# Attention into mixture of experts: router's 32-bit matmuls regrouped, scale sums in bfloat16, low halves of x queued after the maxima

## The chip, the cores and the metric

The kernel runs on one core of one Trainium2 chip. The metric is device time in microseconds (us), the median of several executions; a profile of one execution goes with it. Engines are called PE (TensorE), DVE (VectorE), ACT (ScalarE), POOL (GpSimd) and SP (SyncE, which here only issues DMAs).

## The reference

An attention over 8 batches and 8 heads (1152 keys, head size 64, queries averaged in pairs to 576 rows) feeds a router and eight experts. Every token goes to the expert with the largest logit.

```python
q_pool = q.reshape(B, H, S // factor, factor, D).mean(axis=3)
scores = scale * np.matmul(q_pool, k.transpose(0, 1, 3, 2))
scores = scores - np.max(scores, axis=-1, keepdims=True)
attn = np.exp(scores)
attn = attn / (np.sum(attn, axis=-1, keepdims=True) + 1e-09)
attn_out = np.matmul(attn, v)
...
logits = x @ w_gate
e_idx = np.argmax(logits, axis=1)
...
eom = 1.0 / (1.0 + np.exp(-(x @ w_output_gate)))
for e in range(E):
    mask = e_idx == e
    h = np.maximum(x[mask] @ w1[e], 0.0)
    out[mask] = gate_w[mask, None] * eom[mask, e, None] * (h @ w2[e])
```

Since the choice of the expert is discrete, the attention is computed to nearly 32-bit accuracy: operands are split into a high and a low 16-bit half, and the halves' products are added.

## The kernel before

The attention works on 32 pairs of heads, four pairs to a batch. A loop of steps (18 steps to a pair) writes, in each step, a piece of several generators, and the order in which it writes them is the order on PE, DVE, ACT and POOL (a hand-made order; only SP's DMAs are placed by the scheduler). A step holds:

- the scores of one block of 128 keys (lines 440 and 442) into one of two PSUM buffers `sps`, and their exponentials on ACT (444). In some steps ACT computes a second exponential (446) and DVE subtracts (449) to get the low half `pl`; in the others POOL does it (452);
- one or two row maxima of the next pair (generator `mgen`): two or three matmuls into a PSUM bank `mp` (377) and a DVE reduction (378). Even steps hold one maximum, odd steps two;
- in even steps a burst of up to three blocks of `av`, the product with the values (467 to 469), and at a head's end its division on DVE (476 to 478);
- preparation of the pair after next, by tables of (place, operation), three places to a step: `PREPK` for keys and queries, `PREPV` for values. In it `gk` (213) and `gmax` (319) add a column over the partitions by a 32-bit matmul with a block of ones, and DVE makes a power of two of the sum (218 to 223, 324 to 329). `FWD` moves tables against each other, `SLEAD` is how many steps early the preparation runs.

After a pair's second head the router's generator `logits` takes over, one piece in each even step. For the pair's 128 columns of x it transposes two, then three blocks into PSUM (523, called T2 and T3 here), copies the high half out on ACT (`xh`, 527), subtracts it on DVE for the low half (`xl`, 530), and multiplies both halves by the router's weights in 32-bit matmuls (540), for the columns 0 to 256 (540a) and 256 to 576 (540b) apart, which DVE adds up in `lT` (542, 544). After a batch's fourth pair `router` does the rest. `rows` transposes the maxima in 32 bits (412) once for each group of tiles.

All of 377, 213, 319, 412, 523, 540 and the router's later matmuls share three PSUM banks. `psum()` gives the bank that was given longest ago and isn't held; the writing matmul then waits until DVE or ACT has read what was in it. `psum(True)` holds a bank until `free` is called. Small DVE operations wait in a list `fill`, from which `pop` takes them at fixed points.

After the attention, 21 tiles of tokens go through the experts, in an order that waits for nothing of the above but the last batch's router.

Of the kernel before, what the change touches and what calls it, by code (L numbers as in the profile page):

```python
# [8 lines left out]
F32 = mybir.dt.float32  # L9
F32R = mybir.dt.float32r  # L10
F16 = mybir.dt.float16
BF16 = mybir.dt.bfloat16
# [15 lines left out]
         (78, 'amax', 0), (82, 'amax', 1), (99, 'gmax'), (100, 'scale', 0), (100, 'scale', 1), (100, 'scale', 2), (103, 'vh', 0), (103, 'vs', 0), (106, 'vh', 1), (107, 'vl', 0), (109, 'vs', 1), (113, 'vl', 1))  # L28
PREPK = ((0, 'lk'), (12, 'qsum'), (14, 'kabs'), (20, 'gk'), (21, 'ksc', 0), (22, 'ksc', 1), (23, 'ksc', 2), (25, 'ks', 0), (26, 'ks', 1), (27, 'kh', 0), (29, 'kh', 1), (29, 'kl'), (29, 'qs'), (30, 'dk', 0), (31, 'dk', 1), (31, 'qh'), (33, 'dq', 0), (34, 'dq', 1), (34, 'ql'), (37, 'qd'), (38, 'dl', 0), (40, 'dl', 1))
PREPV = ((63, 'lv'), (82, 'amax', 0), (88, 'amax', 1), (93, 'gmax'), (94, 'scale', 0), (95, 'scale', 1), (99, 'scale', 2), (100, 'vh', 0), (101, 'vs', 0), (103, 'vl', 0), (107, 'vh', 1), (107, 'vs', 1), (110, 'vl', 1))  # L30
FWD = 9
PREP = PREPK + tuple((r + FWD, *x) for r, *x in PREPV)
# [17 lines left out]
P32 = 10  # L50
SLEAD = 35
S = 1152
# [20 lines left out]
def attention(tc, qT, kT, vL, wg, keep, xrows, idscr, cum, pairs, setup, scat, init, exps):  # L73
    nc = tc.nc
    nb = len(pairs) // 4
    with ExitStack() as ctx:
# [16 lines left out]
        def psum(hold=False, name="tp"):  # L93

            while len(held) == 3:
                pop() if fill else pendv.pop(0)()
            k = next(i for i in banks if i not in held)
            free(k)
            if hold:
                held.add(k)  # L100
            x = ps_m.tile([128, 512], F32, name=name, tag=f"mp{k}")
            return (x, k) if hold else x
# [14 lines left out]
        blk = keep['blk']  # L117
# [25 lines left out]
        def prep(n, table):  # L143
# [67 lines left out]
            def gk():  # L211
                g, k_ = psum(True)
                nc.tensor.matmul(g[:, 0:1], lhsT=blk, rhs=ak[:, 0:1], start=True, stop=True)
                gk_.extend((g[:, 0:1], k_))
# [101 lines left out]
            def gmax():  # L316
                g, gk = psum(True)
                g = g[:, 0:2]
                nc.tensor.matmul(g, lhsT=onesf, rhs=am, start=True, stop=True)
                gm.extend((g, gk))  # L320
# [72 lines left out]
        def pop(k=1):  # L393
            while k and fill:
                fill.pop(0)()
                k -= 1
# [87 lines left out]

        routers = []

# [25 lines left out]
        def logits(b, c, xb):  # L512
# [4 lines left out]
            if b == nb - 1 and c == 3:  # L517
                idle(ps_s.tile([128, 512], F32, name="idle4", tag="sps0"), WARM[4])
            for c0, c1, grp in ((0, 256, (0, 1)), (256, NQ, (2, 3, 4))):
                tx, tk = psum(True)  # L520
                for i, t in enumerate(grp):
# [3 lines left out]
                for o, w in ((0, c1 - c0),) if c0 == 0 else ((0, 256), (320, 64)):  # L525
# [3 lines left out]
                    def sub(o=o, w=w, z=z, tx=tx, tk=tk if not d else None):  # L529
                        nc.vector.tensor_tensor(out=xl[:, z], in0=tx[:, o:o + w], in1=xh.bitcast(F32)[:, z], op=ALU.subtract)  # L530
                        if tk is not None:
                            free(tk)
                    fill.insert(0, sub)
                    d += w
                yield 1
            for c0, c1 in ((0, 256), (256, NQ)):
                pop(99)
                tl = psum()
# [147 lines left out]
        with tc.manual_schedule(engines={E.PE, E.DVE, E.Activation, E.Pool}):  # L686
# [19 lines left out]
            for s in range(18 * NP + 14):  # L706
# [8 lines left out]
                for r in routers:  # L715
                    if not s % 2 or not live or not r[1]:
                        r[1] = next(r[0], 0)
                pop()
                if live:
# [6 lines left out]
                adv('m', mg, mw)  # L726
                if s < 54 or s % 2 == 0:
                    rows()
# [6 lines left out]
                if not live:  # L735
                    pop(3)
            pop(99)
            for r in routers:
                for _ in r[0]: pass


def keep_tiles(tc, kp, NT, NP_):
# [8 lines left out]
    nc.vector.memset(t('onesf', [128, 128], F32), 1.0)  # L751
    blk = t('blk', [128, 128], F32)
    nc.gpsimd.memset(blk, 0.0)
# [502 lines left out]
```

## Time and profile before

| | us |
|---|---|
| median of 3 runs | 1487.44 |
| lowest and highest run | 1484.61, 1488.31 |
| profiled execution, whole time | 1491.79 |
| its span, first to last instruction | 1489.9 |
| PE busy in the span | 1431.0 |
| DVE, ACT, POOL busy | 1117.9, 1012.9, 939.1 |

A matmul's end in the profile is modelled: a row maximum's matmul of 384 columns is shown 0.33 us long, but in a dense stretch the next one starts 0.165 us after it. So PE's own time is read from start to start, and an idle time that the profile shows is some 0.16 us shorter than what was lost. PEld rows are weight loads, which overlap with matmuls. The attention takes up to about 983 us of the span, the experts the rest.

### The profile page before, as it was taken

Reading aid. Unit: us, or ns where it says so; the run is one execution under the profiler, and the core shown is the slowest. Engines: PE = TensorE matmul, PEld = TensorE weight load, DVE = VectorE, ACT = ScalarE, POOL = GpSimd, SP = SyncE. Lnnn points to the kernel's source line nnn. Section 1 sums busy time; section 2 is a strip of 40 time slices with the busy share of each in tenths; the row PEclk is TensorE's granted clock in tenths of the full one; section 3 lists DMA queues with packets and bytes.
Section 4 is the critical chain, followed back from the end, with each engine's and each line's share of the span. In section 5 each row is a group of like instructions: output and inputs, shape, how many; then the busy total and the mean of one; then the engine's idle time right before and its main releaser. Section 6 shows DMA issues by size and latency. Waiting matters only on the chain. (4 is left out here: it accounts for less than half of the span.)

```text
span 1489.9 us, 40217 instructions
## 1 busy us (share of the span) xinstructions
PE 1431.0 (96%) x16044; PEld 1144.2 (77%) x16044; DVE 1117.9 (75%) x2438; ACT 1012.9 (68%) x1723; POOL 939.1 (63%) x892
## 2 busy tenths in 40 slices
PE   7899999999999999999999999889999999999996
PEld 4677777777777777777777777777888888888874
DVE  8678787887887787788787787576778778777752
ACT  5777778777877877777877776644655556556542
POOL 3877888788889779878879888663333233333200
PEclk9999999999999999999999999999999999999998
DMA  5445344444443453444244433148636665453550
GB/s 190 123 122 145 102 134 123 115 118 118 117 137 102 115 143 98 117 134 121 86 137 125 126 92 96 58 148 330 231 105 232 228 233 213 171 186 122 218 186 8
DMA packets 92047, 212.57 MB, mean 143 GB/s; under 512 B 13356, under 2 KB 28924, under 8 KB 91854
## 3 DMA queue, kind: packets, MB, share of 16 engines
q1 hardware_dynamic: 81262, 188.35, 40.8%
q0 software_dynamic: 9152, 20.85, 4.1%
q8 instruction: 128, 2.10, 0.6%
q10 hardware_dynamic: 1440, 0.74, 0.2%
q14 instruction: 65, 0.53, 0.1%
HBM read 164.23 MB, written 23.02 MB: 126 GB/s over the span
## 5 line engine op out<-in xcount | busy, mean ns | idle before, releaser
L378 DVE TENSOR_REDUCE pm<-mp 128x1 f32<-128x384 f32 x864 | 449.5, 549 | 114.2 <-PE mp L377 109.6
L444 ACT ACTIVATE p<-sps 128x576 f32<-128x576 f32 x576 | 375.8, 653 | 199.6 <-PE sps L442 180.7
L452 POOL TENSOR_TENSOR pl<-p 128x576 f16<-128x576 f32 x383 | 437.8, 1146 | 112.5 <-ACT p L444 94.0
L377 PE MATMUL mp<-ka,qa 128*128 128x384 f16 x960 | 297.3, 326 | 12.0 <-DVE pm L378 6.5
L467 PE MATMUL av<-vt,p 128*128 128x65 f16 x2880 | 291.8, 193 | 0.2 <-DVE xb L478 0.2
L468 PE MATMUL av<-vt,p 128*128 128x64 f16 x2880 | 291.5, 194 | 0.0
L469 PE MATMUL av<-vt,pl 128*128 128x65 f16 x2880 | 291.1, 192 | 0.0
L467 PEld LDWEIGHTS <-p 128*128 128x128 bf16 x2880 | 265.8, 97 | 20.8 <-DVE xb L478 4.4
L468 PEld LDWEIGHTS <-p 128*128 128x128 bf16 x2880 | 264.4, 97 | 14.0
L469 PEld LDWEIGHTS <-pl 128*128 128x128 f16 x2880 | 264.3, 98 | 0.0
L377 PE MATMUL mp<-kb,qb 66*128 66x384 f16 x768 | 250.7, 326 | 0.8 <-DVE kb L251 0.5
L440 PE MATMUL sps<-qa,ka 128*128 128x288 f16 x1152 | 235.9, 286 | 11.2 <-DVE pl L449 9.8
L958 PE MATMUL hps<-x,w1h 128*128 128x512 f32 (+1 forms) x704 | 230.7, 389 | 7.6 <-DVE x L942 3.4
L442 PE MATMUL sps<-qb,kb 69*128 69x288 f16 x1152 | 235.7, 285 | 0.0
L449 DVE TENSOR_TENSOR pl<-sps,p 128x576 f16<-128x576 f32 x193 | 146.2, 757 | 38.1 <-ACT sps L446 29.8
L958 PE MATMUL hps<-x,w1l 128*128 128x256 f32 (+1 forms) x704 | 165.4, 276 | 0.0
L960 ACT COPY hs<-hps 128x512 f32<-128x512 f32 (+1 forms) x88 | 49.0, 557 | 171.0 <-PE hps L958 171.0
L958 PEld LDWEIGHTS hps<-x,w1l 128*128 128x128 f32 x704 | 132.3, 190 | 13.0
L958 PEld LDWEIGHTS hps<-x,w1h 128*128 128x128 f32 x704 | 122.8, 190 | 23.9 <-DVE x L942 4.0
L442 PEld LDWEIGHTS <-kb 69*128 69x128 f16 x1152 | 112.7, 98 | 29.2
L377 PEld LDWEIGHTS <-qa 128*128 128x128 f16 x960 | 95.2, 99 | 46.8 <-issue 9.5
L790 POOL DMA_INDIRECT ids<-idscr,riD x36 | 44.8, 1244 | 134.4 <-DMA out_dram<-y,ids 123.1
(243 smaller groups left out, 2810.5 us busy)
## 6 DMA issues: line engine op xcount, KB each, us to landing
raw2b<-in_w_dram SPq DMA_DIRECT2D x24, 1024.0 KB
raw1b<-in_w_dram SPq DMA_DIRECT2D x24, 1024.0 KB
raw1a<-in_w_dram SPq DMA_DIRECT2D x22, 1024.0 KB
raw2a<-in_w_dram SPq DMA_DIRECT2D x22, 1024.0 KB
vp<-in_vL_dram SPq DMA_DIRECT2D x32, 576.0 KB
qp<-in_qT_dram SPq DMA_DIRECT2D x31, 576.0 KB
kpf<-in_kT_dram SPq DMA_DIRECT2D x31, 576.0 KB
ka<-xk SPq DMA_DIRECT2D x120, 144.0 KB
```

The source lines that it names most:

```text
L377: nc.tensor.matmul(mp, lhsT=l, rhs=r, start=j == 0, stop=j == len(ops) - 1)
L378: nc.vector.tensor_reduce(out=pm[:, i:i + 1], in_=mp, axis=AX.X, op=ALU.max)
L440: nc.tensor.matmul(sps[:, j, 0:288], lhsT=ka[:, h, ks], rhs=qa[:, o + 288 * j:o + 288 * j + 288], start=True, stop=False)
L442: nc.tensor.matmul(sps[:, j, 0:288], lhsT=kb[:, h, ks], rhs=qb[:, h, 288 * j:288 * j + 288], start=False, stop=True)
L444: e_ = nc.scalar.activation(out=p32.rearrange("p (j n) -> p j n", j=2), in_=x, func=AF.Exp, scale=1.0 / 16)
L449: nc.vector.tensor_tensor(out=pl.rearrange("p (j n) -> p j n", j=2), in0=x, in1=ph.rearrange("p (j n) -> p j n", j=2), op=ALU.subtract)
L452: nc.gpsimd.tensor_tensor(out=pl, in0=p32, in1=ph, op=ALU.subtract)
L467: nc.tensor.matmul(av_[:, qb, 0:65], lhsT=hi, rhs=vt[:, h, c, 0:65], start=c == 0 and qb == 0, stop=False)
L468: nc.tensor.matmul(av_[:, qb, 0:64], lhsT=hi, rhs=vt[:, h, c, 66:130], start=False, stop=False)
L469: nc.tensor.matmul(av_[:, qb, 0:65], lhsT=lo, rhs=vt[:, h, c, 0:65], start=False, stop=c == NC - 1 and qb == 4)
L958: nc.tensor.matmul(hp[:, f, 0:n], lhsT=W1[l][g][:, c, fs], rhs=d['x'][:, c, 0:n], start=c == 0 and l == 0, stop=c == 3 and l == 0)
L960: nc.scalar.copy(out=hs, in_=hp[:, :, w:2 * w])
```

## The change

`gk` and `gmax` take the upper 16 bits of their 32-bit operand as bfloat16, and their ones are bfloat16. In `logits` T3 and 540a are issued in one piece; the subtractions go to a list `subs` that is emptied at the end of a step, after its maxima. `rows` is called, from step 54 on, right behind the router's piece. The K side of the preparation runs a step earlier (`SLEAD` 36, with `FWD` 12 holding the V side where it was), but its low half `kl` on POOL is put one place later than before, behind one more of the step's own subtractions.

```diff
-... (29, 'kh', 1), (29, 'kl'), (29, 'qs'), (30, 'dk', 0), ... (34, 'dq', 1), (34, 'ql'), (37, 'qd'), (38, 'dl', 0), (40, 'dl', 1))
+... (29, 'kh', 1), (29, 'qs'), (30, 'dk', 0), ... (34, 'dq', 1), (33, 'kl'), (35, 'ql'), (38, 'qd'), (41, 'dl', 0), (43, 'dl', 1))
-FWD = 9
+FWD = 12
-SLEAD = 35
+SLEAD = 36
...
             while len(held) == 3:
-                pop() if fill else pendv.pop(0)()
+                subs.pop(0)() if subs else pop() if fill else pendv.pop(0)()
...
-                nc.tensor.matmul(g[:, 0:1], lhsT=blk, rhs=ak[:, 0:1], start=True, stop=True)
+                nc.tensor.matmul(g[:, 0:1], lhsT=blk, rhs=ak.bitcast(BF16)[:, 1:2], start=True, stop=True)
...
-                nc.tensor.matmul(g, lhsT=onesf, rhs=am, start=True, stop=True)
+                nc.tensor.matmul(g, lhsT=ones, rhs=am.bitcast(BF16).rearrange('p (h t) -> p h t', t=2)[:, :, 1], start=True, stop=True)
...
             for c0, c1, grp in ((0, 256, (0, 1)), (256, NQ, (2, 3, 4))):
+                while subs:
+                    subs.pop(0)()
                 tx, tk = psum(True)
...
-                    fill.insert(0, sub)
+                    subs.append(sub)
                     d += w
-                yield 1
+                if c0 == 0:
+                    yield 1
             for c0, c1 in ((0, 256), (256, NQ)):
+                while subs and c0:
+                    subs.pop(0)()
                 pop(99)
...
+                if s >= 54 and s % 2 == 0:
+                    rows()
                 pop()
...
                 adv('m', mg, mw)
-                if s < 54 or s % 2 == 0:
+                while subs:
+                    subs.pop(0)()
+                if s < 54:
                     rows()
```

Place 1, PE, a pair's T3 (`tp<-ident,xb` x3) in the middle of the attention; `tp<-xh,wgt` is 540, `sps` are scores, `mp` maxima. Before:

```order
5400 L377 MATMUL mp_4811<-ka_126,qa_129 128x384
5401 L377 LDWEIGHTS qd_134
5402 L377 MATMUL mp_4811<-kp_3662,qd_134 128x384
5403 L523 MATMUL tp<-ident,xb 128x128 x3
5404 L440 LDWEIGHTS ka_125
5405 L440 MATMUL sps_4827<-qa_128,ka_125 128x288
```

Now:

```order
5417 L377 LDWEIGHTS qd_134
5418 L377 MATMUL mp_4811<-kp_3647,qd_134 128x384
5419 L525 MATMUL tp<-ident,xb 128x128 x3
5420 L545 MATMUL tp<-xh,wgt 128x256
5421 L545 MATMUL tp<-xl,wgt 128x256
5422 L440 LDWEIGHTS ka_125
5423 L440 MATMUL sps_4833<-qa_128,ka_125 128x288
```

540a, which stood two steps later by itself, follows T3 with no score or maximum between; two steps on, 540b and the transposes 412 stand together in the same way.

Place 2, DVE, the steps of T2 and T3 of a pair (`pm` is a maximum, `xl` a subtraction of x, `pl` one of the exponentials). Before:

```order
535 L378 TENSOR_REDUCE pm<-mp_6057 128x1
536 L449 TENSOR_TENSOR pl<-sps_6045,p_6043 128x576
537 L530 TENSOR_TENSOR xl<-tp,xh 128x256
538 L378 TENSOR_REDUCE pm<-mp_6081 128x1
539 L378 TENSOR_REDUCE pm<-mp_6130 128x1
540 L378 TENSOR_REDUCE pm<-mp_6138 128x1
541 L449 TENSOR_TENSOR pl<-sps_6121,p_6119 128x576
542 L530 TENSOR_TENSOR xl<-tp,xh 128x64
543 L378 TENSOR_REDUCE pm<-mp_6162 128x1
```

Now:

```order
535 L378 TENSOR_REDUCE pm<-mp_6064 128x1
536 L449 TENSOR_TENSOR pl<-sps_6048,p_6046 128x576
537 L378 TENSOR_REDUCE pm<-mp_6085 128x1
538 L532 TENSOR_TENSOR xl<-tp,xh 128x256
539 L378 TENSOR_REDUCE pm<-mp_6133 128x1
540 L378 TENSOR_REDUCE pm<-mp_6138 128x1
541 L449 TENSOR_TENSOR pl<-sps_6126,p_6124 128x576
542 L385 TENSOR_REDUCE m_6143<-pm 128x5
543 L549 TENSOR_TENSOR lT<-tp,lT 32x256
```

The subtraction of T2 stands behind the even step's maximum instead of before it. On ACT, in front of T2's copy `xh`, before:

```order
309 L227 ACTIVATE kpf<-kpf,ik 128x576 x2
310 L444 ACTIVATE p_5379<-sps_5381 128x576
311 L446 ACTIVATE sps_5381<-sps_5381 128x2x288
312 L276 CAST xk_5043<-kpf 128x576 x2
313 L230 ACTIVATE qs<-qs,ik 128x576
314 L527 CAST xh<-tp 128x256
```

Now:

```order
310 L276 CAST xk_5025<-kpf 128x576 x2
311 L230 ACTIVATE qs<-qs,ik 128x576
312 L444 ACTIVATE p_5382<-sps_5384 128x576
313 L446 ACTIVATE sps_5384<-sps_5384 128x2x288
314 L285 CAST xq<-qs 128x576
315 L529 CAST xh<-tp 128x256
```

The three long operations of the K side have moved in front of the exponentials of the step before T2; the shorter `xq` has come in.

Place 3, DVE, `gk`'s scale (`tp<-tp`, `ik`) at the end of a batch, where the division (`r`, `xb`) stands too. Before:

```order
594 L476 TENSOR_SCALAR r<-av_6397,sc 128x5
595 L477 RECIPROCAL r<-r 128x5
596 L478 TENSOR_TENSOR xb<-av_6397,r 128x5x64
597 L218 TENSOR_SCALAR tp<-tp 128x1
598 L378 TENSOR_REDUCE pm<-mp_6686 128x1
599 L220 TENSOR_SCALAR ik<-tp 128x1
```

Now:

```order
596 L218 TENSOR_SCALAR tp<-tp 128x1
597 L378 TENSOR_REDUCE pm<-mp_6627 128x1
598 L220 TENSOR_SCALAR ik<-tp 128x1
599 L223 RECIPROCAL ik<-ik 128x1
600 L632 TENSOR_REDUCE tp<-r_6589 128x5
601 L634 TENSOR_TENSOR posi<-tp,moob 128x5
602 L476 TENSOR_SCALAR r<-av_6404,sc 128x5
```

The scale, at whose end the held bank of `gk` is freed, stands a step before the division instead of behind it.

## Rows read from the trace of the kernel before

**Rows 1.** The page, part 1 (busy time, share of the span, instructions).

```profile
PE 1431.0 (96%) x16044; PEld 1144.2 (77%) x16044; DVE 1117.9 (75%) x2438; ACT 1012.9 (68%) x1723; POOL 939.1 (63%) x892
```

**Rows 2.** Busy time by stretch: stretch, its length, busy time and number of instructions of PE, PEld, DVE, ACT and POOL, granted clock of PE, DMA share and GB/s. The first is a whole batch, from its first T2 to the next batch's; the second lies among the experts.

```profile
312.47:429.50 117.03, 114.98 (x1667) 89.96 (x1667) 93.28 (x245) 91.39 (x167) 96.67 (x91) 1.00 0.44 119
...
1102.70:1104.50 1.80, 1.80 (x14) 1.57 (x13) 1.80 (x2) 0.88 (x3) 0.00 (x0) 1.00 0.03 9
```

**Rows 3.** PE's waits from 100 to 940 us: who waited for whom, us in total, times, longest.

```profile
PE mp L377 <- DVE pm L378: 6.3, 13, 0.6
PE mp L377 <- DVE xl L530: 3.7, 14, 0.3
PE tp L523 <- DVE pm L378: 2.7, 9, 0.3
PE sps L440 <- DVE pl L449: 1.2, 2, 1.0
PE mp L377 <- DVE ik L220: 0.6, 1, 0.6
PE tp L540 <- DVE pm L378: 0.3, 1, 0.3
```

**Rows 4.** PE's timeline around a pair's T2 and T3: start, duration, instruction, in brackets the idle time before it and who ended it.

```profile
252.89 0.38 PE L523 MATMUL tp<-ident,xb 128*128 128x128 f32 x2
...
255.49 0.49 PE L377 MATMUL mp<-ka,qa 128*128 128x384 f16 x2
255.82 0.32 PE L377 MATMUL mp<-kp,qd 128*128 128x384 f16 x1
256.40 0.48 PE L377 MATMUL mp<-ka,qa 128*128 128x384 f16 x2 [0.26 <-DVE xl L530]
```

**Rows 5.** DVE's timeline over the same steps.

```profile
255.93 0.42 DVE L530 TENSOR_TENSOR xl<-tp,xh 128x256 fp32r<-128x256 f32 x1 [1.26 <-ACT xh L527]
256.27 1.48 DVE L378 TENSOR_REDUCE pm<-mp 128x1 f32<-128x384 f32 x3
258.20 0.76 DVE L449 TENSOR_TENSOR pl<-sps,p 128x576 f16<-128x576 f32 x1 [0.46 <-ACT sps L446]
```

**Rows 6.** ACT's timeline over the same steps.

```profile
253.16 0.65 ACT L446 ACTIVATE sps<-sps 128x576 f32<-128x576 f32 x1
253.73 1.23 ACT L276 CAST xk<-kpf 128x576 f16<-128x576 f32 x2
254.86 0.78 ACT L230 ACTIVATE qs<-qs,ik 128x576 f32<-128x576 f32 x1
255.54 0.36 ACT L527 CAST xh<-tp 128x256 fp32r<-128x256 f32 x1
256.33 0.68 ACT L285 CAST xq<-qs 128x576 f16<-128x576 f32 x1
```

**Rows 7.** PE's timeline around `gk` at the end of a batch, and around the next T2.

```profile
306.91 0.36 PE L213 MATMUL tp<-ak,blk 128*128 128x1 f32 x2
307.13 0.41 PE L440 MATMUL sps<-qa,ka 128*128 128x288 f16 x2
...
307.79 0.33 PE L377 MATMUL mp<-kb,qb 66*128 66x384 f16 x1
308.76 0.32 PE L377 MATMUL mp<-ka,qa 128*128 128x384 f16 x1 [0.65 <-DVE pm L378]
...
311.82 0.33 PE L377 MATMUL mp<-kb,qb 66*128 66x384 f16 x1
312.47 0.44 PE L523 MATMUL tp<-ident,xb 128*128 128x128 f32 x2 [0.32 <-DVE pm L378]
```

**Rows 8.** DVE's timeline around the same `gk`.

```profile
307.60 0.49 DVE L478 TENSOR_TENSOR xb<-av,r 128x320 f32<-128x320 f32 x1
...
308.63 0.15 DVE L220 TENSOR_SCALAR ik<-tp 128x1 f32<-128x1 f32 x1
```

**Rows 9.** PE's timeline around a `gmax`, and around the router's small bfloat16 matmuls.

```profile
323.36 0.28 PE L319 MATMUL tp<-am,onesf 128*128 128x2 f32 x2
323.51 0.32 PE L377 MATMUL mp<-ka,qa 128*128 128x384 f16 x1
...
304.61 0.24 PE L601 MATMUL tp<-ohb,ones 128*128 128x32 bf16 x4
304.71 0.18 PE L602 MATMUL tp<-cum,ones 128*128 128x40 bf16 x1
```

**Rows 10.** PE's timeline at a 540a among the 16-bit matmuls, and at eight transposes among the experts' 32-bit matmuls.

```profile
202.05 0.33 PE L377 MATMUL mp<-kb,qb 66*128 66x384 f16 x1
...
202.46 0.42 PE L440 MATMUL sps<-qa,ka 128*128 128x288 f16 x2
...
1103.05 1.04 PE L939 MATMUL xps<-ident,xg 128*128 128x128 f32 x8
...
1104.16 0.40 PE L981 MATMUL yp<-w2l,hh 128*128 128x512 f32 x1
```

**Rows 11.** The queues that the K side is moved past: POOL's wait for `xk` before `kl`, and SP's and ACT's timelines of one load of the values and its first use.

```profile
POOL kp L279 <- ACT xk L276: 60.8, 22, 10.1
...
275.14 0.33 SPq L272 DMA_DIRECT2D vp<-in_vL_dram  x1
...
287.55 0.73 ACT L314 ACTIVATE junk<-vp 128x576 f16<-128x576 f32 x1
```

More of the change, by code (lines that the diff above doesn't have):

```diff
@@ L28 @@
          (78, 'amax', 0), (82, 'amax', 1), (99, 'gmax'), (100, 'scale', 0), (100, 'scale', 1), (100, 'scale', 2), (103, 'vh', 0), (103, 'vs', 0), (106, 'vh', 1), (107, 'vl', 0), (109, 'vs', 1), (113, 'vl', 1))
-PREPK = ((0, 'lk'), (12, 'qsum'), (14, 'kabs'), (20, 'gk'), (21, 'ksc', 0), (22, 'ksc', 1), (23, 'ksc', 2), (25, 'ks', 0), (26, 'ks', 1), (27, 'kh', 0), (29, 'kh', 1), (29, 'kl'), (29, 'qs'), (30, 'dk', 0), (31, 'dk', 1), (31, 'qh'), (33, 'dq', 0), (34, 'dq', 1), (34, 'ql'), (37, 'qd'), (38, 'dl', 0), (40, 'dl', 1))
+PREPK = ((0, 'lk'), (12, 'qsum'), (14, 'kabs'), (20, 'gk'), (21, 'ksc', 0), (22, 'ksc', 1), (23, 'ksc', 2), (25, 'ks', 0), (26, 'ks', 1), (27, 'kh', 0), (29, 'kh', 1), (29, 'qs'), (30, 'dk', 0), (31, 'dk', 1), (31, 'qh'), (33, 'dq', 0), (34, 'dq', 1), (33, 'kl'), (35, 'ql'), (38, 'qd'), (41, 'dl', 0), (43, 'dl', 1))
 PREPV = ((63, 'lv'), (82, 'amax', 0), (88, 'amax', 1), (93, 'gmax'), (94, 'scale', 0), (95, 'scale', 1), (99, 'scale', 2), (100, 'vh', 0), (101, 'vs', 0), (103, 'vl', 0), (107, 'vh', 1), (107, 'vs', 1), (110, 'vl', 1))
-FWD = 9
+FWD = 12
 PREP = PREPK + tuple((r + FWD, *x) for r, *x in PREPV)
@@ L483, in av @@
             yield
-        routers = []
+        routers, subs = [], []
         wf = bp.tile([128, 4, 16], F32, name="wf")
@@ L737, in attention @@
             pop(99)
+            while subs:
+                subs.pop(0)()
             for r in routers:
@@ L751, in keep_tiles @@
     nc.vector.memset(t('onesf', [128, 128], F32), 1.0)
-    blk = t('blk', [128, 128], F32)
+    blk = t('blk', [128, 128], BF16)
     nc.gpsimd.memset(blk, 0.0)
```

## The prediction, made before the changed kernel ran

> **What bounds the kernel now.** I read the page's busy times first: PE is busy for 96% of the span, the next engine, DVE, for 75% [rows 1]. Busy shares mix stages, so the second view is busy time by stretch: over one whole batch in the steady middle PE is busy 114.98 of 117.03 us at a granted clock of 1.00, that is at its upper level of 2.4 GHz, while POOL has 96.67, DVE 93.28 and ACT 91.39 [rows 2]. PE bounds the attention, and there are two ways to shorten it: to give it less work, or to take away its waits. The third view, PE's waits from 100 to 940 us, says who holds it up: almost always DVE, by way of the three shared PSUM banks [rows 3]. The fourth, the timelines of PE, DVE and ACT side by side, shows why. The reader is to look at starts, since a matmul's shown end hides about 0.16 us of each wait.
>
> **What the waits are worth.** Rows 3 has five lines in which a maximum, a T2 or T3 or a 540 waits for DVE: 6.3 + 3.7 + 2.7 + 0.6 + 0.3 = 13.6 us in 13 + 14 + 9 + 1 + 1 = 38 waits [rows 3]. With 0.16 us hidden in each, 13.6 + 38 x 0.16 = 19.7 us. The timelines show three kinds of them:
>
> - Behind T2. T2 starts at 252.89 [rows 4], but its copy `xh` starts on ACT at 255.54 only, behind the second exponential, two `xk` and `qs` [rows 6]. DVE, in order, stands for 1.26 us before `xl`, with the maximum of T2's own step behind it [rows 5]. So the bank of that maximum stays full, and the third maximum starts at 256.40 where 255.82 + 0.165 = 255.99 was due: 0.42 us lost [rows 4].
> - Behind `gk` at a head's end. The division (`xb` from 307.60 to 308.09) stands on DVE before the scale, whose `ik` at 308.63 frees `gk`'s bank [rows 8]. On PE the next maximum starts at 308.76 instead of 307.95: 0.81 us [rows 7]. It is the largest single wait.
> - Before a batch's first T2: 312.47 instead of 311.98, 0.49 us, since the router gives back its held bank only in that very step [rows 7].
>
> **The change part by part, against the profiled execution.**
>
> *Sums in bfloat16.* A 32-bit `gk` is two matmuls and takes PE from 306.91 to 307.13, 0.22 us [rows 7]; a `gmax` from 323.36 to 323.51, 0.15 us [rows 9]. A small bfloat16 matmul takes about 0.03 us: four of them from 304.61 to 304.71 [rows 9]. Per pair 0.19 + 0.12 = 0.31 us, for 32 pairs **9.9 us**. Not shown is such a matmul with a weight of its own among large ones. The lower bound is 0.025 us (those four), the upper 0.11 us, a transpose's share of T2 (0.22 us for two to the scores, and eight in rows 10 go at the same pace) [rows 9, 10]: gains of 10.2 down to 32 x (0.37 - 0.22) = 4.8 us. I take the first, the nearer row, since it too has small operands. The Trainium skill has a rule on this, in "TensorE: Matmul & The Clock Gate", section "Weight-path perf modes": the fast weight load is for types other than FP32, and by the section on LDWEIGHTS before it a plain load of 128 columns takes about 107 ns. By that rule each sum would lose two such loads, and the gain would be an estimated 2 x 32 x (0.21 - 0.025) = 12 us. The trace agrees for `gk` and not for `gmax`, whose two matmuls take 0.15 us with all their loads [rows 9]; I stay with the rows.
>
> *32-bit matmuls together.* 540a alone takes PE from 202.05 + 0.165 to 202.46, 0.245 us [rows 10]. The eight transposes and a 32-bit matmul of 512 columns take 1104.16 - 1103.05 = 1.11 us; at 0.11 us a transpose the matmul has 0.23, which is 0.115 us for 256 columns and 0.23 for the two of 540a [rows 10]. So changing over between 16 and 32 bits costs at most 0.015 us, and 32-bit transposes next to 32-bit matmuls cost nothing extra. I value this edit by itself at **0**; its bounds are 0.03 us either way at two places of 32 pairs, 2 us.
>
> *Waits removed.* With the subtraction behind the even step's maximum (place 2) that maximum's bank is read at once, and the wait behind T2 goes. It is helped on ACT: ahead of `xh` stood 0.65 + 1.23 + 0.78 = 2.66 us, now an exponential of the same 0.65 before, one more of 0.65 and `xq` of 0.68, 1.98 us [rows 6]. With `gk` a step earlier the scale comes before the division (place 3), so its bank is free before the division's 0.49 us and its short companions hold DVE up. The router, whose 540a has no step of its own any more, gives its bank back two steps earlier, before the next T2. All three kinds are named by the order on DVE, so I take the whole **19.7 us** as gone, and 2 us more for the start of the attention (before 100 us) and for waits shorter than 0.16 us, which don't show as idle.
>
> *Waits added.* T3 now holds one bank, 540a takes a second right behind it, and 540b and the transposes 412 do the same two steps later. The bank that the second one gets is that of the odd step's first maximum. That maximum's two matmuls start 0.165 us apart, the second is shown 0.33 us long, then DVE reads for 0.55 us (1.48 us for three in a row is 0.49 each at least [rows 5]): about 1.0 us after its start. The two maxima take 0.66 us, T3 0.33, so 540a could start at 0.99, and the transposes behind 540b at about 0.95. An estimated 0.1 us each, if DVE has nothing else before: 64 x 0.1 = **6.4 us** back. Bounds: nothing, where the maximum is one of three matmuls and the cover longer; and 0.42 us at each of the 64 places, the wait of rows 4, 27 us. Behind a late 540a nothing else waits on PE but what is behind it in order, which is all.
>
> *K side a step earlier, `kl` a place later.* POOL stood 60.8 us in 22 times before `kl`, waiting for `xk` [rows 11]; one more of the step's own subtractions goes into that time. On SP the load `qp` passes in front of `vp`; `vp` went out at 275.14 and is first read at 287.55 [rows 11], so 12.4 us cover a swap that is worth one load. Both at 0. Without that cover ACT would wait for the values; it has 117.03 - 91.39 = 25.6 us free in a batch [rows 2], 6.4 us a pair, before that reaches PE.
>
> *The experts* keep their order; nothing is counted there.
>
> Sum: 9.9 + 19.7 + 2 - 6.4 = 25.2 us. The profiled execution took 1491.79 us, so it would take 1466.6. It was 4.35 us over the median of the runs, 1487.44, which becomes **1462**.
>
> **The rivals.**
>
> 1. *The waits only change place.* `xl` still waits for `xh`, and behind it now stand the two maxima of the odd step. For it: in rows 4 to 6 `xl` would end near 256.3 and the odd step's first maximum is ready at 255.49 + 0.49 + 0.16 = 256.14, so there is hardly cover. Against it: `xh` has 0.7 us less before it, and a bank read 0.2 us late is needed only two maxima on. Then 540a's bank waits eat up the rest of the gain and the sums alone remain: 1487.4 - 9.9 = 1478.
> 2. *Slower: DVE's waits for `xh` pass on to PE in full.* DVE stands 1.26 us before T2's `xl` and 0.46 us in T3's step [rows 5]. Today a burst of `av` and a score hide most. It decides when `xl` ends more than about 0.4 us after the odd step's first maximum is ready: then with T3's bank held both free banks are full, and PE stands for as long as DVE did, 1.72 us in each of 32 pairs, 55 us. Against that stand the 29.6 us of the sums and the old waits: 1487 + 25 = 1512. Against it speaks the shorter queue on ACT.
> 3. *More than forecast.* The added bank waits are nothing: 1487.4 - 31.6 = 1456, and with the waits of the second `sps` buffer (1.2 us [rows 3]) and cheaper changes-over down to 1452.
> 4. *The freed time isn't usable*, because another engine sets the pace: no change, 1487. Against it: POOL, the next, has 96.67 us in a batch, and PE would need 117.03 - 25.2 / 8 = 113.9 [rows 2].
> 5. *The clock.* The Trainium skill says in "TensorE: Matmul & The Clock Gate", "Part 4: PE-mode transpose", that transposes don't count as busy for the clock, so longer groups of them could let it fall. The row speaks against: over the experts' eight transposes in a row the granted clock is 1.00 [rows 2]. If it did, T2, T3, 540 and 412 (some 1.3 us of a pair: 0.22 + 0.33 + 0.245 + 0.245 x 320 / 256 + 2 x 0.11) would go at 1.2 GHz and take double, 42 us more than the forecast, 1504.
>
> **How the numbers follow.** Forecast 0.69 (its own range 1453 to 1472), waits that only change place 0.13, more than forecast 0.09, no usable time 0.03, slower by DVE 0.05, the clock 0.01. For 8 in 10, the forecast, the larger gain and the first rival's place at 1478: **1449 to 1479**; the low end takes in cheaper changes-over and sums at their best. A measurement here tells about 0.3%, 4.5 us, from no change. The first three give faster: 0.91. Same: 0.03. The two slower ones: 0.06.
>
> **What would show it.** In the profile after: `gk` and `gmax` with one weight load each and about 0.03 us from their start to the next; no idle time of PE put down to `xl` in front of `mp`; a maximum behind `gk` at 0.165 us; small waits (0.1 us) before 540a and 412 instead; a batch of about 114 us. Wrong would be a batch over 116 us, PE waits before 540a or the odd maxima of over 0.3 us in every pair, or DVE idle before `xl` as long as now with maxima behind it.

## The result, and the profile after

The changed kernel took 1507.38 us (median of 4 runs, 1504.76 to 1509.41) where the kernel before took 1487.43 beside it: a ratio of 1.0136, 95% interval 1.0113 to 1.0160. It is slower; forecast were 1462, and 1449 to 1479 as the range. The page, part 1, of the changed kernel, whose profiled execution took 1509.41 us with a span of 1507.6, answers to [rows 1]:

```profile
PE 1433.2 (95%) x15980; PEld 1137.6 (75%) x15980; DVE 1116.2 (74%) x2438; ACT 1017.1 (67%) x1723; POOL 940.3 (62%) x892
```

There are 64 matmuls fewer, and the busy time of every engine is within 0.5% of that before; so the new time is idle time, or time between starts that the shown lengths of matmuls hide. The batch of [rows 2], from its first T2 to the next batch's (stretch, length, busy times of PE, PEld, DVE, ACT and POOL, clock, DMA share, GB/s):

```profile
317.06:437.13 120.07, 115.31 (x1660) 89.30 (x1659) 93.14 (x245) 92.29 (x168) 96.87 (x92) 1.00 0.42 117
```

It is 3.04 us longer than the 117.03 before, at the same granted clock. Single batches of one kernel differ (117.0 to 119.4 us before, 119.5 to 120.6 now), so kernels are compared by the seven batches from the first T2 of the first to that of the eighth; before and now they are

```profile
75.97:900.11 824.14, 806.65 (x11672) 629.88 (x11670) 654.11 (x1719) 640.81 (x1166) 675.45 (x637) 1.00 0.43 119
```

```profile
76.92:916.82 839.90, 809.00 (x11615) 625.05 (x11614) 652.06 (x1720) 643.51 (x1165) 675.75 (x636) 1.00 0.42 118
```

which is 15.8 us more, 2.25 us a batch, and nearly all of the 17.7 us by which the span grew. PE's waits from 100 to 940 us, for [rows 3]:

```profile
PE sps L440 <- DVE pl L449: 19.9, 47, 0.7
PE mp L377 <- DVE pm L378: 4.9, 8, 0.7
PE tp L213 <- DVE pm L378: 2.3, 7, 0.3
PE tp L412 <- DVE pm L378: 1.2, 7, 0.2
PE tp L525 <- DVE pm L378: 0.5, 2, 0.3
```

Of the waits that the forecast struck off, two kinds are nearly gone: no maximum waits for `xl` any more (14 times before), and T2's waits have fallen from 2.7 to 0.5 us. The kind behind `gk` has only moved: maxima still wait 4.9 us for `pm`, once a batch 0.65 us while DVE does the division (at 301.31 us in the batch of the lines below), and `gk` itself now waits 0.3 us once a batch. Beside them scores wait for DVE's `pl`, 19.9 us where there were 1.2. The timelines of ACT, DVE and PE around a T2 (start, duration, instruction; it is the place of [rows 4 to 6]) show how. ACT:

```profile
254.91 1.24 ACT L276 CAST xk<-kpf 128x576 f16<-128x576 f32 x2
256.05 0.78 ACT L230 ACTIVATE qs<-qs,ik 128x576 f32<-128x576 f32 x1
256.72 0.64 ACT L444 ACTIVATE p<-sps 128x576 f32<-128x576 f32 x1
257.25 0.65 ACT L446 ACTIVATE sps<-sps 128x576 f32<-128x576 f32 x1
```

DVE:

```profile
258.01 0.76 DVE L449 TENSOR_TENSOR pl<-sps,p 128x576 f16<-128x576 f32 x1 [1.26 <-ACT sps L446]
```

PE, from the end of block 7's score to block 9's, and on to T3 and 540a:

```profile
254.94 0.41 PE L442 MATMUL sps<-qb,kb 69*128 69x288 f16 x2
...
255.85 0.38 PE L525 MATMUL tp<-ident,xb 128*128 128x128 f32 x2
...
258.82 0.42 PE L440 MATMUL sps<-qa,ka 128*128 128x288 f16 x2 [0.69 <-DVE pl L449]
...
260.30 0.49 PE L525 MATMUL tp<-ident,xb 128*128 128x128 f32 x3
260.72 0.36 PE L545 MATMUL tp<-xh,wgt 128*128 128x256 f32 x1
260.91 0.28 PE L545 MATMUL tp<-xl,wgt 128*128 128x256 f32 x1
261.03 0.42 PE L440 MATMUL sps<-qa,ka 128*128 128x288 f16 x2
```

Block 7's scores are complete at 254.94 + 0.41 = 255.35, but ACT, in order, has two `xk` and `qs` first and starts the exponential at 256.72. Block 7 is one of those with a second exponential, which overwrites the scores in their own buffer, and DVE reads them there last, from 258.01. Block 9 uses the same buffer and waits for that. DVE's own idle time has moved from one to the other: before, it stood 32.3 us for `xh` and 14.5 for the second exponential (DVE's waits from 100 to 940 us),

```profile
DVE xl L530 <- ACT xh L527: 32.3, 28, 1.3
DVE pl L449 <- ACT sps L446: 14.5, 30, 1.7
```

and now 0.9 and 31.8:

```profile
DVE pl L449 <- ACT sps L446: 31.8, 30, 1.3
DVE xl L532 <- ACT xh L529: 0.9, 1, 0.9
```

It is less in sum, 32.7 us after 46.8, but at `pl` PE stands right behind it.

The second thing shows no idle time at all, only starts. T3's three transposes go at 0.109 us, so the third starts at 260.52. From there to the score are 0.51 us with 540a between (261.03 - 260.52); before, T3's last transpose to a score was 0.11 and 540a between a maximum and a score added 0.24 (202.46 - 202.05 - 0.165 [rows 10]), together 0.35. The same happens two steps on, where 540b and the transpose 412 stand together:

```profile
264.09 0.31 PE L545 MATMUL tp<-xl,wgt 128*128 128x320 f32 x1
264.42 0.28 PE L412 MATMUL tp<-ident,m 128*5 128x128 f32 x1
264.53 0.41 PE L440 MATMUL sps<-qa,ka 128*128 128x288 f16 x2
```

540b's second matmul is followed after 0.33 us by the transpose; a score follows it after 0.15 in the kernel before. Medians over the steady part (315 to 940 us) give 0.167 us more at the first place and 0.183 at the second: 0.35 us a pair, 1.40 a batch, 11.2 for the 32 pairs.

Both are waits for a bank, too short to show as idle time of PE. 540a gets the bank of the odd step's first maximum (the order in which `psum` gives them), which DVE reads here:

```profile
260.01 0.56 DVE L378 TENSOR_REDUCE pm<-mp 128x1 f32<-128x384 f32 x1 [0.45 <-PE mp L377]
```

The reduction ends at 260.57, and 540a starts 0.15 us later. In the changed kernel and in experiments 4, 6, 8 and 9 it starts 0.145 to 0.148 us after the end of that reduction in all 150 pairs in which maxima still run, while its distance from T3's last transpose varies from 0.197 to 0.370 us. At the second place the profile names the wait, at the transpose's weight load:

```profile
263.81 0.56 DVE L378 TENSOR_REDUCE pm<-mp 128x1 f32<-128x384 f32 x1 [0.72 <-PE mp L377]
```

```profile
264.42 0.08 PEld L412 LDWEIGHTS tp<-ident,m 128*5 128x5 f32 x1 [0.29 <-DVE pm L378]
```

In all 28 places of this kind in the changed kernel the transpose starts 0.054 or 0.055 us after the end of the reduction, as far behind as in the waits for `pm` that show in the kernel before (0.054 to 0.058). Behind the last maximum of the attention no reduction is under way, and there T3 and 540a stand together like this, matmuls and weight loads:

```profile
975.97 0.49 PE L525 MATMUL tp<-ident,xb 128*128 128x128 f32 x3
976.22 0.36 PE L545 MATMUL tp<-xh,wgt 128*128 128x256 f32 x1
```

```profile
976.19 0.19 PEld L545 LDWEIGHTS tp<-xh,wgt 128*128 128x128 f32 x1
...
976.53 0.10 PEld L440 LDWEIGHTS <-ka 128*128 128x128 f16 x1
```

The third transpose starts at 976.19, the router's weights are loaded from that moment on, 540a starts 0.03 us later, and the next score's weights, whose load elsewhere starts with the score (at 261.03 above), are loaded 0.346 us behind the transpose: the 0.35 us of the kernel before. So 32-bit matmuls standing together cost nothing by themselves here.

Before that was seen, the theory to test was the other reading, that they do, together with a score's wait; the rivals were that the K side's new order alone is to blame, and that any wait removed comes back in another place.

### The profile page after: what moved, and what is told of

Read it like the earlier page. It is cut to its first block, busy times and chain, and to the rows that moved or that the text cites. A ratio compares the mean times of both kernels' runs of the same rounds, so it can differ in the third digit from the quotient of the medians.

```text
span 1507.6 us, 40020 instructions
## 1 busy us (share of the span) xinstructions
PE 1433.2 (95%) x15980; PEld 1137.6 (75%) x15980; DVE 1116.2 (74%) x2438; ACT 1017.1 (67%) x1723; POOL 940.3 (62%) x892
## 5 line engine op out<-in xcount | busy, mean ns | idle before, releaser
L440 PEld LDWEIGHTS <-ka 128*128 128x128 f16 x1152 | 86.9, 97 | 59.5 <-DVE pl L449 31.7
```

Source lines behind the costliest of these rows:

```text
L440: nc.tensor.matmul(sps[:, j, 0:288], lhsT=ka[:, h, ks], rhs=qa[:, o + 288 * j:o + 288 * j + 288], start=True, stop=False)
```

## The experiments

Ratios are to the kernel before, run beside each on the same chip; its median was 1491.0 to 1493.2 us in these runs, 4 to 6 us above the value beside the changed kernel, so ratios or batches are compared, not bare times.

**1. The sums alone** (`gk`, `gmax` and `blk` as in the change).

```diff
-... lhsT=blk, rhs=ak[:, 0:1], ...
+... lhsT=blk, rhs=ak.bitcast(BF16)[:, 1:2], ...
```

> The kernel before with the two sums in bfloat16 and nothing else. From the trace after, gk costs PE 0.03 us instead of 0.22 and gmax 0.03 instead of 0.15: every theory expects 32 x 0.31 = 10 us less than before (about 1477). If the time stays, PE's saved work isn't on the path.

1487.93, ratio 0.9962 (0.9948 to 0.9976): 5.7 us, little over half of the forecast term. `gk` gives what was forecast: it and the gap behind it fall from 0.221 to 0.027 us, 0.19 a pair. `gmax` gives nothing. PE's timeline there:

```profile
353.25 0.17 PE L319 MATMUL tp<-am,ones 128*128 128x2 bf16 x1
353.39 0.32 PE L377 MATMUL mp<-ka,qa 128*128 128x384 f16 x1
```

The maximum behind it still starts 0.14 us after `gmax`, where the two 32-bit matmuls took 0.15 [rows 9]. In the changed kernel the same gap is 0.029, so a small bfloat16 matmul does cost that little. Here the maximum waits for its bank, below what the profile shows as idle time: it starts 0.05 us after the end of DVE's reduction

```profile
352.79 0.55 DVE L378 TENSOR_REDUCE pm<-mp 128x1 f32<-128x384 f32 x1
```

and 0.053 to 0.055 us after it in 26 of 28 places between 100 and 940 us, in the kernel before as well. 32 x 0.19 = 6.2 us is about what was measured.

**2. The K side alone** (with the new `PREPK`).

```diff
-FWD = 9
+FWD = 12
-SLEAD = 35
+SLEAD = 36
```

> The kernel before with the K side a step earlier and kl a place later, nothing else. Theory A (on ACT xk, xk and qs now stand before the odd step's two exponentials, so pl and with it the sps buffer come late): a wait of 0.8 us of sps for pl two us after T2 in most pairs, some 20 us more, less up to 10 us for gk before the division: 5 to 20 us slower than before. Theory B (the slowdown is in the banks, held by T3 and 540a at once): no slower than before, rather 5 to 10 us faster.

1492.38, ratio 0.9993 (0.9981 to 1.0005). Neither faster nor slower, and yet all its waits are others:

```profile
PE sps L440 <- DVE pl L449: 13.4, 20, 0.7
...
PE mp L377 <- DVE pm L378: 0.2, 1, 0.2
```

The waits of the maxima are gone (6.3 us for `pm` in [rows 3], 0.2 here; one for `xl` is left of 14) and the score's wait for `pl` has come. So the K side brings the wait seen in the changed kernel, but pays for it with those that it removes, and cannot be the whole loss.

**3. Sums and subtractions behind the maxima.**

```diff
-                    fill.insert(0, sub)
+                    subs.append(sub)
...
                 adv('m', mg, mw)
+                while subs:
+                    subs.pop(0)()
```

> The kernel before with the sums in bfloat16 and the subtractions behind the step's maxima; T3 and 540a apart, rows and K side as before. Theory A: 10 us less for the sums, 6 to 8 us less for the waits behind T2: about 1471. Theory C (the subtractions behind the maxima make pl late): not under 1477, sps waits for pl of about 0.8 us two us after T2.

1488.11, ratio 0.9977 (0.9960 to 0.9993): the same as the sums alone. The wait behind T2 that [rows 4] shows is gone, and its time stands elsewhere:

```profile
PE mp L377 <- DVE pm L378: 9.0, 14, 0.8
PE sps L440 <- DVE pl L449: 5.4, 20, 1.0
```

**4. All but the K side** (the whole diff without `PREPK`, `FWD` and `SLEAD`).

> The changed kernel with the K side as before. Theory A: the sps waits for pl two us after T2 go, and with them some 15 to 20 us; what stays against the kernel of e3 is the price of 32-bit matmuls standing together, 0.17 and 0.18 us a pair, 11 us: about 1482. Theory B: still slower than before, above 1495.

1508.41, ratio 1.0102 (1.0079 to 1.0126): as slow as the whole change within the intervals. What it has more than experiment 3 is the regrouping, so this kernel's loss comes with that. It isn't all the changed kernel's loss: here 540b, too, starts late (0.39 us behind a maximum's start, 0.03 in the changed kernel), and in three of the seven batches the granted clock was at its lower level, 1.2 GHz, for a short stretch, where the changed kernel has 1.00 throughout. With 540b late, 412 follows its second matmul after 0.15 us in 24 of 28 pairs, as a score does.

**5. All but the regrouping** (T3 and 540a in two pieces, 412 at its old place, K side moved).

> The kernel before with the sums in bfloat16, the subtractions of x behind the maxima and the K side's new places; T3 and 540a stay in two pieces and the transposes of the maxima where they stood. Theory A (the slowdown sits in the 32-bit matmuls put together): no slower than before, 1480 to 1492 us beside a before of 1488 to 1493, ratio 0.993 to 1.001, and no step of the pair in which PE has 0.20 us between a transpose of x and the router's matmul. Theory B (the subtractions behind the maxima are harmless alone, and so is the K side, but together they queue too much on ACT two steps behind T2): as slow as the change, 1503 to 1510, ratio above 1.008. Either way I expect a wait of the score two steps behind T2 for DVE's pl of some 0.5 to 0.9 us in three of four pairs.

1489.10, ratio 0.9969 (0.9955 to 0.9983), as theory A forecast. The expected wait of the score is there in full, 13.4 us in 20 visible waits, and the kernel is still not slower than before. Its seven batches:

```profile
75.07:897.49 822.42, 800.30 (x11615) 625.20 (x11613) 652.38 (x1719) 640.80 (x1165) 675.17 (x636) 1.00 0.43 119
```

**6. T3 and 540a together, 412 at its old place, K side as before.** To experiment 3 is added:

```diff
-                yield 1
+                if c0 == 0:
+                    yield 1
...
-                while subs:
+                while subs and c0:
```

> Sums in bfloat16, subtractions behind the maxima, T3 and 540a in one piece; the transposes of the maxima at their old place at the step's end, the K side as before. Beside it stand the kernel without that one piece (1488.1, ratio 0.998) and the one with the transposes moved as well (1508.4, ratio 1.010). Theory A1 (T3 with 540a is the whole of it): 1502 to 1509, ratio 1.007 to 1.012. Theory A2 (the transposes of the maxima behind 540b are the whole of it): 1485 to 1491, ratio below 1.000. Half and half: 1494 to 1501. In PE's order T3's last transpose to 540a should read 0.20 us in this kernel, and 540b to the next score 0.15 instead of 0.33 to a transpose.

1508.57, ratio 1.0102 (1.0085 to 1.0119): moving 412 back gains nothing, against A2. But A1 doesn't hold as it was meant either, since T3 with 540a is dearer by only 32 x 0.167 = 5.3 us, and this kernel lost 20 against experiment 3. Most of the rest are waits, because the router is now a piece earlier: 540b, two steps earlier and nearer to what it reads, starts late,

```profile
263.27 0.33 PE L377 MATMUL mp<-kb,qb 66*128 66x384 f16 x1
263.67 0.39 PE L545 MATMUL tp<-xh,wgt 128*128 128x320 f32 x1
```

0.40 us behind the maximum's start where experiment 5 has 0.03, for 32 pairs an estimated 11.7 us by the medians (0.394 and 0.028); and the maxima stand longer for DVE, 14.5 us where experiment 3 has 9.0:

```profile
PE mp L377 <- DVE pm L378: 14.5, 21, 1.2
```

A part is the clock. In four of the seven batches the granted clock was at 1.2 GHz for a short stretch (0.986 over the batch); the two of these in the middle took 120.3 and 120.5 us, the three at 1.00 118.8 to 119.3. That is an estimated 6 us in four batches, and experiment 3 has 1.00 in all seven.

**7. A bfloat16 matmul between T3 and 540a,** in the changed kernel, in three of a batch's four pairs: of 1, 128 and 1 columns, issued behind ACT's copy of T3's bank, and in the last of these pairs one more of 1 column between 540a's two.

```diff
+                if c0 == 0 and c:
+                    nc.tensor.matmul(tx[:, 384:512] if c == 2 else tx[:, 384:385], lhsT=ones, rhs=ones if c == 2 else ones[:, 0:1], start=True, stop=True)
                 pop(99)
...
+                    if c == 3 and j == 0 and c0 == 0:
+                        nc.tensor.matmul(tl[:, 384:385], lhsT=ones, rhs=ones[:, 0:1], start=False, stop=False)
```

> The changed kernel with small bfloat16 matmuls of ones (into unused columns) between T3 and 540a: in a batch's first pair none, in the second one of 1 column, in the third one of 128 columns, in the fourth one of 1 column and another between 540a's two matmuls. Now it is 0.200 + 0.194 + 0.122 = 0.516 us from T3's last transpose to the score behind 540a; the kernel before had 0.109 + 0.240 for the same work apart. Theory C (a 32-bit matmul right behind another 32-bit one pays extra): with 1 column between, the 0.516 falls to about 0.38 to 0.42. Theory D (the router's 32-bit weights are loaded beside the matmul ahead of them, and a transpose or a column is too short to hide that): with 1 column the sum stays at 0.50 to 0.58, with 128 columns it is 0.45 to 0.55 although 0.05 us of work are added. Each dummy's own price is 0.03 us (1 column) or 0.055 (128). The time itself should stay within 3 us of the changed kernel's.

1528.59 in one run, and a failed experiment: the added matmul writes into the bank that ACT's copy reads, and as it came after the copy it started 0.85 us behind T3's last transpose, 0.74 later than its turn; 24 times that is 18 us. What can be read from it is that behind such a wait 1 or 128 columns made no difference to 540a. The experiment was repeated, as the ninth, with the matmul ahead of the copy.

**8. The changed kernel with another block for the second exponential.**

```diff
-PLP = (1, 3, 7, 9, 11, 13)
+PLP = (1, 3, 5, 9, 11, 13)
```

> The changed kernel with one number of the table of second exponentials altered: block 5 instead of block 7 of each pair has its low half from ACT and DVE, block 7's comes from POOL. The work of every engine stays the same. Now PE stands 0.5 us on average in each pair for the score of block 9, which waits for DVE's subtraction of block 7's second exponential (18 us of the run), since ACT also has x's high half, the query sums and xk in those steps. Theory E (these waits come from ACT's queue at that place): that wait goes, some 10 to 18 us are won, 1490 to 1498, ratio to before 0.998 to 1.005. Theory F (waits only change place, since some engine is late in every pair by that much): another wait of the same size appears, two to six steps off, and the time stays within 4 us of 1507, ratio 1.010 to 1.016.

1487.44, ratio 0.9953 (0.9936 to 0.9969): 20 us less than the changed kernel by one number (seven batches take 839.90 and 820.87 us, 19.0 less), more than E forecast; by the ratios it would be 27, since the kernels before beside the two differ by 6. ACT around T2, which here starts at 252.72:

```profile
252.35 1.24 ACT L276 CAST xk<-kpf 128x576 f16<-128x576 f32 x2
253.48 0.78 ACT L230 ACTIVATE qs<-qs,ik 128x576 f32<-128x576 f32 x1
254.16 0.64 ACT L444 ACTIVATE p<-sps 128x576 f32<-128x576 f32 x1
```

and PE's waits:

```profile
PE mp L377 <- DVE pm L378: 4.9, 8, 0.6
PE sps L440 <- DVE pl L449: 4.4, 23, 0.4
```

The queue of `xk` and `qs` is the same, but block 7's scores are now free when its one exponential ends, without a second and without DVE. The score's wait falls from 19.9 to 4.4 us, and no other takes its place, against F.

**9. The same again, ahead of ACT's copy:** 1, 128 and 64 columns in a batch's second to fourth pair.

```diff
                     nc.tensor.transpose(out=tx[:, 128 * i:128 * i + 128], in_=x, identity=ident)
+                if c0 and c:
+                    w = (0, 1, 128, 64)[c]
+                    nc.tensor.matmul(tx[:, 384:384 + w], lhsT=ones, rhs=ones[:, 0:w], start=True, stop=True)
```

> The changed kernel again with a bfloat16 matmul of ones behind T3, this time issued ahead of ACT's copy, so that it waits for nothing: none in a batch's first pair, 1 column in the second, 128 in the third, 64 in the fourth. In the run before it each of them waited 0.85 us for ACT, and behind it 540a's two matmuls stood 0.198 apart whether 1 or 128 columns were ahead. Now: 0.200 from T3's last transpose to 540a. Theory C (a 32-bit matmul pays for standing right behind a 32-bit transpose): transpose to dummy 0.11, dummy to 540a 0.03, 540a to its second 0.194 to 0.255: a sum that is lower by 0.05 or more than 0.516 less the dummy. Theory D (loading the router's 32-bit weights takes a time of its own, which only a long matmul ahead covers): transpose to dummy 0.11, dummy to 540a so much that the sum is 0.51 to 0.55 with 1 column, and it grows with 64 and 128 columns by less than their 0.03 and 0.055 us. The time stays within 3 us of the changed kernel's 1507.

PE's timeline in a pair with 1 column:

```profile
230.86 0.49 PE L525 MATMUL tp<-ident,xb 128*128 128x128 f32 x3
231.19 0.17 PE L528 MATMUL tp<-ones 128*128 128x1 bf16 x1
231.28 0.35 PE L548 MATMUL tp<-xh,wgt 128*128 128x256 f32 x1
```

From T3's last transpose to the added matmul it is 0.109 us and from there to 540a 0.090, 0.199 together, with 1, 64 and 128 columns alike (5 pairs each); without it 0.200. The added matmuls cost nothing at their place, 128 columns included. That falls against theory C: what stands right ahead doesn't matter. Theory D's figures are met, but not its reason: 128 columns cover nothing of the load. What stays the same is the distance from DVE's reduction, 0.145 to 0.148 us to 540a here too. In the pair in which that ended later (540a at 830.99 us, 0.304 behind T3's last transpose), the added matmul kept its 0.109 and 540a moved with the reduction. So the added matmuls stand in the time of a wait for a bank. The run's 1515.11 is a single time. One pair (825.9 to 861.6 us) took 35.7 us where the changed kernel took 29.7; the granted clock was 0.83 between 840 and 860 us, partly the lower level of 1.2 GHz, behind 20 us in which PE was busy for 17.69. The other pairs keep the changed kernel's pace, and why this one didn't is open.

**10. All but the regrouping, with block 5:** the kernel of experiment 5 with the edit of experiment 8.

> All of the change but the regrouping (T3 and 540a in two pieces, the transposes of the maxima at their old place), and block 5 instead of block 7 with ACT's second exponential. Without the altered table it took 1489.1 (ratio 0.997), with 17 us of waits for block 9's scores between 100 and 900 us; the changed kernel lost 20 us by the same alteration. Theory E (those waits are ACT's queue at that place) and theory G (the 32-bit islands cost the changed kernel 11 us, and some 7 us of waits six steps behind T3 besides): 1468 to 1476, ratio 0.983 to 0.989. Theory F (waits only change place): 1484 to 1490, ratio 0.994 to 0.998.

1471.15, ratio 0.9858 (0.9833 to 0.9883), the fastest of all: 1.4% under the kernel before and, by the two ratios, 2.7% under the changed one (0.9858 / 1.0136 = 0.973), or 2.4% by the bare times. Its seven batches:

```profile
74.53:878.27 803.74, 796.69 (x11616) 623.65 (x11614) 653.17 (x1719) 636.16 (x1164) 675.20 (x636) 1.00 0.44 122
```

**11. The kernel before, with the edit of experiment 8 and nothing else.**

> The kernel before with block 5 instead of block 7 for ACT's second exponential and nothing else. Before, block 9's scores wait for nothing, and the waits stand in the steps of blocks 5, 6 and 9 (4.9, 3.1 and 7.8 us between 200 and 900 us), behind gk's sum and behind T2. If the table of block 5 fits only the new places of the K side: 1488 to 1500, ratio 0.997 to 1.005. If it is better by itself, whatever the change does: 1475 to 1484, ratio 0.988 to 0.994, and then the change would have to be judged against this one.

1479.95, ratio 0.9926 (0.9900 to 0.9951): the table is better by itself. PE's waits have no line of a maximum for `xl` any more; an exponential less stands ahead of `xh` on ACT and a subtraction less ahead of `xl` on DVE, and which of the two does it was not told apart. Its seven batches:

```profile
75.20:887.42 812.22, 800.80 (x11672) 630.94 (x11670) 650.71 (x1719) 642.92 (x1166) 676.32 (x637) 1.00 0.44 121
```

**12. The changed order of steps with block 5, its 32-bit matmuls apart.** 540a goes out in T3's step, but behind that step's maximum, and 412 at the step's end.

```diff
+                if c0 == 0:
+                    late.append(prod)
...
                     adv('m', mg, pos['m'] + 1)
+                while late:
+                    late.pop(0)()
```

> The changed kernel with block 5 in the table, and with its 32-bit matmuls in the same steps as in the change but not adjacent: 540a is issued in T3's step behind that step's maximum, and the transposes of the maxima stand at the step's end again. So the router still ends a piece earlier than in the kernel before, only the 32-bit matmuls have other work ahead of them. The changed kernel with block 5 took 1487.4 (ratio 0.995), the one with 540a a step of its own 1471.2 (0.986). Theory D (0.167 us for T3 with 540a and 0.183 for 540b with the transposes, 11 us over 32 pairs, because only a long matmul ahead covers the loading of 32-bit weights): 540a begins 0.03 us behind the maximum, and the time is 1473 to 1479, ratio 0.987 to 0.991. Theory H (the 16 us come mostly from the router's work being a piece earlier, which crowds steps 9 and 11 and leaves step 13 too short for ACT): 1481 to 1488, ratio 0.992 to 0.996, with the wait for block 15's scores (6 us between 200 and 900 us) still there in both cases.

1476.14, ratio 0.9891 (0.9872 to 0.9910), the time and the place of 540a that theory D gave. PE at 540a:

```profile
254.77 0.33 PE L377 MATMUL mp<-kb,qb 66*128 66x384 f16 x1
254.80 0.42 PE L546 MATMUL tp<-xh,wgt 128*128 128x256 f32 x1
```

This doesn't bear out D's reason, since a free bank gives the same: 540a comes a maximum later and 412 at the step's end, when DVE has read their banks. The size had been taken from the starts, whatever their cause. The seven batches of this kernel and of experiment 8 (the second) differ by this alone:

```profile
76.47:886.75 810.28, 796.10 (x11616) 623.46 (x11614) 653.33 (x1720) 635.80 (x1164) 673.47 (x636) 1.00 0.44 122
```

```profile
76.35:897.22 820.87, 805.22 (x11615) 623.64 (x11614) 653.50 (x1720) 638.87 (x1164) 674.62 (x636) 1.00 0.43 120
```

(820.87 - 810.28) / 7 = 1.51 us a batch, where four pairs of the 0.35 us read from the starts make 1.40.

## Why the prediction was wrong, point by point

Seven batches of each kernel, read in one profiled execution each and all at a granted clock of 1.00, split the loss. Sums, subtractions and K side, which were to gain most, take them from 824.14 to 822.42 us (experiment 5): -0.25 a batch, where 9.9 + 19.7 + 2 = 31.6 us, or 3.95 a batch, were forecast for them together with the wait before a batch's first T2. The regrouping then adds 17.48 us, 2.50 a batch, where 6.4 / 8 = 0.8 was forecast. Together that is +2.25 for a forecast of -3.15. With block 5 the parts come apart: sums, subtractions and K side do gain there, 116.03 to 114.82, -1.21 (experiments 11 and 10); the router's work a piece earlier adds 0.93 (10 to 12, to 115.75); the two waits for a bank behind T3 and 540b add 1.51 (12 to 8, to 117.27).

- *K side at 0, and the waits removed counted whole, is the first step that failed.* The prediction counted what stood on ACT ahead of `xh`, found it 0.7 us shorter, and stopped there. The operations that now stand behind `xk` and `qs` are the two exponentials of block 7, and the first of them starts 1.4 us after its scores are complete, as the chain to block 9's score shows. So DVE stands for ACT at `pl`, with PE right behind it: 19.9 us of shown waits in place of 1.2, which eat up what the removed ones gave. Experiment 8 took ACT's second exponential out of that place and won 2.72 us a batch, where the same alteration wins 1.70 in the kernel before. Rival 2 had this shape (DVE's wait for ACT passes on to PE, 1512) but put it at `xl`, where it didn't happen: `xl`'s idle time nearly vanished. That its 1512 lies near the measured time is luck.
- *Waits removed*: the wait behind T2 and the one before a batch's first T2 were named rightly and went. The one at the division stays, at 0.65 us a batch as before, though `gk`'s scale now comes earlier: DVE's division still stands between a maximum and its reduction. And a wait taken away gave no time by itself: experiment 3 removed the wait behind T2 and experiment 2 those behind `gk`, and both left the time as it was. Rival 1 said this, with 0.13, but its 1478 has none of the new waits.
- *Waits added, 6.4 us before 540a and 412*, is the second: right in mechanism and place, but too small: 0.167 and 0.183 us were measured for the 0.1 of the sum, 11.2 us, inside the bounds of 0 to 27. At 412 DVE's reading ends 1.09 us after the maximum's start (263.28 to 264.37) where 1.0 was estimated, and the restart takes 0.055 us on top. At 540a the bank comes free only 0.03 us after its turn (260.57 for 260.54), but the restart takes 0.147; why more than elsewhere isn't shown.
- *The router's pieces two steps earlier* had no term but as a gain for T2, the third step that failed. They cost 0.93 us a batch by waits elsewhere in the pair. PE's waits from 100 to 940 us show only part of it: in experiment 12 scores wait 5.1 us for `pl`, maxima 4.9 for `pm` and `gk` 2.3, against 2.8, 0.3 and none in experiment 10, while T2's 2.5 and the router's 2.2 there are nearly gone.
- *32-bit together, valued at 0*, held: behind the last maximum T3 and 540a take together what they took apart, and in experiment 4 a 32-bit transpose follows 540b as closely as a score does.
- *Sums, 9.9 us*: 5.7 measured alone, inside the bounds of 4.8 to 10.2. The price of one was right; `gmax`'s half was hidden behind a wait for a bank, which the kernel before had too, unseen. In the changed kernel both gaps are 0.03 us.
- *Rival 5, the clock*, fell: 1.00 over all seven batches and the span's mean as before, 0.991. *Rival 4* fell too: experiment 10, at 114.82 us for the 117.73 before, shows that 2.9 us a batch could be used.
- *The experts*, with the last batch, took 590.8 us from that batch's first T2 to the end, 589.8 before.

## What to carry to other kernels

When instructions move forward in a queue, price the ones that they now stand in front of, up to whoever waits last for those; the queue of the thing that is to be helped is only half of it. Where several writers share a few banks, set each start beside the end of the read that frees its bank: a short wait shows no idle time, and a distance from that end that never varies tells a wait from a price of the matmul itself. An experiment that comes out at the expected time doesn't prove the reason, if another reason would give the same time. In a kernel whose other engines are 80% busy, a wait removed is worth something only once it is known what would be late next; a small change of a table that fits the new order was worth more here than all of the change's own edits.

## What the runs showed of the hardware

A weight load of 128 columns is 0.19 us long in the profile for the router's 32-bit weights, against 0.10 in 16 bits. Such a load began together with a 32-bit transpose, at 976.19 us in the changed kernel, and together with a maximum's 16-bit matmul, at 202.05 us in the kernel before, and the 540a behind it took as long in both (0.24 us beside the transpose's or the maximum's own time): at neither place did its length cost time.

A matmul or transpose that waits for a bank starts 0.053 to 0.058 us after the end of DVE's reading: in 23 waits for `pm` that show in the kernel before, in the 28 of 412 and behind `gmax` in 26 of 28. 540a behind T3 starts 0.145 to 0.148 us after it. What sets the difference no run shows.
